# LSH attention followed by a feed-forward layer: the first batch's hidden layer by seven half-size products, its operands and all weight block sums made during attention

## The chip, the cores and the metric

The kernel runs on one core of a Trainium2 chip. The metric is the device time of one execution in microseconds (us). The engines are called as in the profile: PE multiplies matrices and writes PSUM, ACT, DVE and POOL work element by element, and SP issues nearly all DMAs. Each engine takes its instructions strictly in order; engines wait for each other through semaphores.

## The reference

Attention runs over 4 batches, 8 heads, 768 tokens and head size 64. Queries and keys are hashed to 6 bits each by the signs of a projection, and a query attends only to the keys of its own bucket. Its output, laid out as 3072 tokens by 512, goes through a feed-forward layer of 2048 hidden values with a piecewise quadratic activation:

```python
q_bits = (np.einsum('bhsd,dk->bhsk', q, proj) > 0)
k_bits = (np.einsum('bhsd,dk->bhsk', k, proj) > 0)
mask = q_bucket[:, :, :, None] == k_bucket[:, :, None, :]
scores = np.where(mask, scale * np.matmul(q, k.transpose(0, 1, 3, 2)), -1e9)
attn = softmax(scores)                  # with 1e-9 added to the sum
x = np.matmul(attn, v)                  # as 3072 x 512
h = x @ w_in                            # 512 x 2048
g = np.where(h >= 1, h, np.where(h <= -1, 0.0, (h + 1) ** 2 / 4))
out = g @ w_out                         # 2048 x 512
```

The weights arrive as 64-bit floats. Every product that needs more than the matrix format's precision is made of three: each operand is split into a high part and a rest, and high by high, rest by high and high by rest are summed.

## The kernel before

**Attention** (`attention`) goes through 32 heads, a pair of heads at a time, in units: a unit is 128 keys by 384 queries, so a head has 12 units and the stage has 384. At unit g, PE makes the scores (lines 378, 379), ACT takes the exponential twice (line 387 rounded to the matrix format, line 392 in full), and one unit later DVE, or POOL for two units in six, subtracts the two and so makes the rest `pl` (line 39 through `lo_unit`). Four units behind, PE multiplies by the values (`pv_unit`, lines 411, 413, 415). For the head after next, PE makes one pair of `smax` products every two units (line 310) into a single buffer, and DVE reduces the buffer to row maxima (line 314); the next pair can be made only when that reduction is done. Everything else is a task that is put behind a numbered unit (`at(g, fn)`), in the order of the code.

**Weights.** A block of 128 hidden values (an f, of which there are 16 for w_in and 16 for w_out) is converted from 64-bit floats by a load, a rescaling on ACT (`rebias`, line 66) and three integer steps on DVE (`tail`, `shifted`, `signed`, lines 70, 74, 78), which use a PSUM bank as scratch. For 12 blocks of w_in, ACT then makes the high part and POOL the rest, into a large resident tile `wbig`. Twelve more blocks (4 of w_in, 8 of w_out) are converted in attention and put to DRAM to be split later. So heads 3 to 26 each carry one conversion.

**Feed-forward.** The tokens go by chunks of 384, two chunks to a batch. The hidden layer of the first batch (chunks 0 and 1) is made directly: 32 steps (`ffn_order`, `gemm1`, line 976) of 12 products for one chunk and one f. The other three batches use the seven-product scheme of Strassen's kind on 2 by 2 blocks (`PRODUCTS`): for a pair of f's and both chunks, seven half-size products of 6 matmuls each (line 1071) give four results that would otherwise take eight such products. Seven block combinations of the weights (`wc`, in DRAM) and of the tokens are its operands; a ring of buffers holds the weight blocks that come next. The results are combined on DVE and ACT (`cm`, `cu`, `cv`, lines 1076 to 1090), go through the activation (`act_in` on ACT, `act_out` on DVE), are split by `g_hi` and `g_lo`, and wait in a list as nine output matmuls each (`queue_out`, line 839, 512 wide). `issue(n)` takes the next n from that list, five or six behind each product.

While the first batch ran in the old way, DVE also made the weight block sums (`w_get`, `w_sum`, `w_hi`, `w_lo`, `w_put`) and the token operands of batch 1 (`x_plan`). The token operands of chunk 0 were made in heads 28 to 31 (`make`: two DVE steps, a POOL copy and a POOL subtraction per block of 128), those of chunk 1 in the first steps of the feed-forward stage.

Two PSUM banks, `h0` and `h1`, take the products in turn. A product that starts afresh in a bank, or accumulates onto the one before it there, has to wait until the engine that reads the earlier result has read it.

Of the kernel before, what the change touches and what calls it, by code (L numbers as in the profile page):

```python
# [41 lines left out]
class WeightSplit:  # L42
# [10 lines left out]
    def steps(self, src, shape, hi, lo, cp, stage=None, low=None, keep=None, word=None):  # L53
        nc, n = self.nc, self.n
        st = {}

# [7 lines left out]
        def rebias():  # L64
            st["sq"] = self.pool.tile([P, n], F32, name="wsq")
            nc.scalar.activation(out=st["sq"], in_=st["raw"][:, :, 1].bitcast(F32), func=AF.Copy, scale=REBIAS)

        def tail():
            a = st["a"] = self.pool.tile([P, n], I32, name="wa", bufs=1) if word is None else word()
            nc.vector.tensor_scalar(out=a, in0=st["raw"][:, :, 0], scalar1=29, scalar2=None,  # L70
                                    op0=ALU.logical_shift_right)
# [10 lines left out]
        def s5():  # L82
            if cp is nc.scalar:
                cp.copy(out=hi, in_=st["sq"])
            else:
                cp.tensor_copy(out=hi, in_=st["sq"])

        def s6():
            sub(nc, low or nc.gpsimd, lo, st["sq"], hi.bitcast(F32))

        def put():
            nc.sync.dma_start(out=keep if stage is None else stage, in_=st["sq"])

        if stage is None:
            return [s0, rebias, tail, shifted, signed, s5, s6] + ([put] if keep is not None else [])

        def get(sq=None):
            st["sq"] = self.pool.tile([P, n], F32, name="wsq") if sq is None else sq
            nc.sync.dma_start(out=st["sq"], in_=stage)

        return [s0, rebias, tail, shifted, signed, put], [get, s5, s6]


# [551 lines left out]
LEAD = 8  # L655
# [7 lines left out]
NRING = 9  # L663
# [3 lines left out]
class XMaker:  # L667
# [23 lines left out]
    def load_sv(self, c, sv):  # L691
        self.sv[c] = sv
        self.nc.sync.dma_start(out=sv, in_=self.x_d[c // 2][:, :, S:S + 2])

# [6 lines left out]
    def load_er(self, c, ct, er):  # L701
        self.load_rows(c // 2, ct, c % 2, er)
        self.er[c, ct] = (er[:, 0], er[:, 1])

    def load_raw(self, c, ct, raw):
        b, sl = c // 2, slice(c % 2 * CH, (c % 2 + 1) * CH)
        self.nc.sync.dma_start(out=raw, in_=self.x_d[b][:, ct, sl])
        self.raw[c, ct] = raw

    def make(self, c, ct, part, hi, lo, eng):  # L710

        nc = self.nc
        r, sv = self.raw[c, ct], self.sv[c]
        eb, rb = self.er[c, ct]
        if part == 0:
            nc.vector.scalar_tensor_tensor(out=r, in0=eb, scalar=sv[:, ct, 0:1], in1=r,
                                           op0=ALU.mult, op1=ALU.add)
        elif part == 1:
            eng[0].tensor_tensor(out=r, in0=r, in1=rb, op=ALU.mult)
        elif part == 2:  # L720
            (nc.scalar.copy if c > 0 else nc.gpsimd.tensor_copy)(out=hi[:, ct], in_=r)
        else:
            sub(nc, eng[1], lo[:, ct], r, hi[:, ct].bitcast(F32))


def ffn_order():


    steps = [(0, f) for f in range(LEAD)]
    for f in range(NFT):  # L730
        steps.append((1, f))
        if f + LEAD < NFT:
            steps.append((0, f + LEAD))
    return steps


def ffn(ctx, tc, wpair, woh, wol, xm, xa, xb, areas, wst, wq, wc, out, prep, post, staged):
# [12 lines left out]
    nc.vector.memset(m1, -1.0)  # L750
    pcs = xp.tile([P, 6, CH], F32, name="pcs")
    pc = [pcs[:, n] for n in range(6)]
    tmp = xp.tile([P, 2, 4, HM], F32R, name="tmp")
    sum_w = xp.tile([P, 4, HM], F32, name="sumw")
    sflat = sum_w.rearrange("p b n -> p (b n)")
    spc = (xp.tile([P, NCT, 2], F32, name="xsva"), xp.tile([P, NCT, 2], F32, name="xsvb"))
    xs = [xa, xb]
    N1 = 2 * NFT
    (ta, tb, tu), big = areas
    tflat = tmp.rearrange("p a b n -> p (a b n)")  # L760

    def cut(t, n):
        return t[:, n * CH:(n + 1) * CH]
# [3 lines left out]
            + [cut(big, n) for n in range(28, 32)] + [cut(tflat, n) for n in range(5)]  # L767
            + [cut(tu, n) for n in range(3)])

    def operand(b, o, cc, t):  # L770
        return sets[(b - 1) % 2][cc * 2 * NBLK + 2 * o + t]

    def spread(b, cc, k):

        if b == 2:
            t, n = (ta, 2 * k) if cc == 0 else ((tb, 6), (big, 28), (big, 30), (tu, 0))[k]
        elif b == 3:
            t, n = big, 2 * NBLK * cc + 2 * k
        else:
            t, n = (ta, 2 * k) if cc == 1 else (tflat, 2 * k) if k < 2 else (sflat, 0) if k == 2 else (  # L780
                pcs.rearrange("p k n -> p (k n)"), 4)
        return t[:, n * CH:(n + 2) * CH].bitcast(F32).rearrange("p (t n) -> p t n", t=2)
# [6 lines left out]

    def mid(n, fn, *a):  # L790

        (prep if n < N1 else post)[n].append((fn, a))

# [22 lines left out]

    def flush(c, m):
# [64 lines left out]
    def x_plan(b, cc, raw, er, norm, made):  # L882

        at(raw, x_raw, b, cc)
        for k, n in enumerate(norm):
            mid(n, x_norm, b, cc, k)
            at(er[k], x_er, b, cc, k)
# [64 lines left out]
    def ring_staged():  # L952
# [4 lines left out]
        for k in range(4):  # L957
            w_load(k)
# [346 lines left out]
```

## Time and profile before

| | |
|---|---|
| median of 3 runs | 968.71 us (968.69 to 968.91) |
| the profiled execution | 968.67 us, of which the span of its instructions is 966.7 us |
| granted PE clock | 0.999 |
| PE, matmuls | 956.6 us busy, 5050 of them |
| DVE, ACT, POOL busy | 747.8, 680.4 and 322.4 us |
| attention | up to 450.55 us of the span |
| first batch's direct steps | 450.55 to about 578.7 us |

Matmuls of PE overlap: one that shows 0.34 us is followed by the next 0.175 us after its start, so the pace is read from the distance of starts, or from the chain of waits, and not from the durations. The same is true on a smaller scale for ACT and DVE, whose instructions start some 0.1 us ahead of the end of the one before.

### The profile page before, as it was taken

How to read it: one execution, taken by the hardware profiler on the slowest of the kernel's cores; microseconds unless marked ns; L12 is line 12 of the kernel's file. 1: busy time of each engine (PE TensorE's matmuls, PEld its weight loads, DVE VectorE, ACT ScalarE, POOL GpSimd, SP SyncE). 2: the span in 40 equal slices, each digit the busy share in tenths (PEclk: the TensorE clock that was granted, in tenths of full speed). 3: DMA queues.
4: the chain of work that ended last, by engine and by line, in shares of the span. 5: the costliest groups of instructions: out<-in, count | busy, mean ns of one | idle time of the engine just before them, and what ended most of it. 6: DMA issues, size and time to landing. Idle time of an engine off the chain costs nothing.

```text
span 966.7 us, 15568 instructions
## 1 busy us (share of the span) xinstructions
PE 956.6 (99%) x5050; PEld 889.8 (92%) x5050; DVE 747.8 (77%) x1313; ACT 680.4 (70%) x1482; POOL 322.4 (33%) x433
## 2 busy tenths in 40 slices
PE   8999999999999999999999999999999999999998
PEld 7899999999999999999889998888998899888996
DVE  8778889888888888885988787787866777655554
ACT  7789999999999999987655465555564545544444
POOL 8777776666677776476000000000000000000000
PEclk9999999999999999999999999999999999999999
DMA  5776656666766666636691669966458554454431
GB/s 160 191 190 161 167 163 181 180 182 201 193 188 172 172 169 169 146 106 166 193 346 45 196 209 314 306 215 190 120 181 217 159 174 120 145 151 119 121 87 65
DMA packets 95112, 167.55 MB, mean 173 GB/s; under 512 B 13956, under 2 KB 51960, under 8 KB 95032
## 3 DMA queue, kind: packets, MB, share of 16 engines
q1 hardware_dynamic: 94762, 166.53, 60.3%
q8 instruction: 40, 0.66, 0.3%
q14 instruction: 40, 0.33, 0.1%
q10 hardware_dynamic: 270, 0.04, 0.0%
HBM read 106.13 MB, written 33.87 MB: 145 GB/s over the span
## 4 chain that ended last, share of the span: by engine, by line
PE 94%; DVE 2%; ACT 1%; issue 0%; ACTq 0%; DVEq 0%
PE y L839 27%; PE h L1071 18%; PE h L976 7%; PE smax L310 7%; PE o L411 7%; PE o L415 7%; PE s L378 7%; PE o L413 7%; PE s L379 6%; PE o L208 2%; DVE nm L314 1%; ACT ph L387 0%; ACT t L798 0%; ACT z L799 0%; PE s L355 0%
## 5 line engine op out<-in xcount | busy, mean ns | idle before, releaser
L387 ACT ACTIVATE ph<-s 128x384 fp32r<-128x384 f32 x380 | 189.7, 499 | 32.7 <-PE s L379 25.2
L314 DVE TENSOR_REDUCE nm<-smax 128x1 f32<-128x768 f32 x189 | 179.6, 950 | 22.5 <-PE smax L310 22.1
L39 DVE TENSOR_TENSOR pl<-s,ph 128x384 fp32r<-128x384 f32 x256 | 137.5, 548 | 28.8 <-ACT s L392 27.8
L39 POOL TENSOR_TENSOR pl<-pf,ph 128x384 fp32r<-128x384 f32 x128 | 129.8, 1014 | 88.2 <-ACT pf L392 85.0
L804 DVE SCALAR_TENSOR_TENSOR t<-t 128x384 f32<-128x384 f32 x128 | 71.3, 557 | 106.4 <-ACT z L799 106.3
L378 PE MATMUL s<-t 128*128 128x384 f32 x384 | 130.5, 340 | 0.0
L411 PE MATMUL o<-ph,va 128*128 128x386 f32 x384 | 130.1, 339 | 0.2 <-DVE neg L219 0.2
L413 PE MATMUL o<-ph,vb 128*128 128x386 f32 x384 | 129.9, 338 | 0.0
L415 PE MATMUL o<-pl,va 128*128 128x386 f32 x384 | 129.9, 338 | 0.0
L379 PE MATMUL s<-t 128*128 128x384 f32 x384 | 129.5, 337 | 0.0
L392 ACT ACTIVATE s<-s 128x384 f32<-128x384 f32 x252 | 126.2, 501 | 0.0
L839 PE MATMUL y<-t,ghi 128*128 128x512 f32 x384 | 124.7, 395 | 0.0
L310 PE MATMUL smax<-t 128*128 128x384 f32 x378 | 99.3, 344 | 2.6 <-DVE nm L314 2.0
L798 ACT ACTIVATE t<-h,mh 128x384 f32<-128x384 f32 x56 | 32.5, 581 | 83.3 <-PE h L976 43.8
L809 ACT CAST ghi<-z 128x384 fp32r<-128x384 f32 x129 | 65.1, 505 | 30.1 <-DVE z L805 26.3
L799 ACT ACTIVATE z<-t,m 128x384 f32<-128x384 f32 x128 | 79.0, 617 | 4.2
L839 PEld LDWEIGHTS y<-t,ghi 128*128 128x128 f32 x384 | 71.3, 188 | 11.1 <-ACT ghi L809 0.3
L1071 PE MATMUL h<-wbig,t 128*128 128x384 f32 x399 | 81.4, 336 | 0.0
L798 ACT ACTIVATE t<-wsq,mh 128x384 f32<-128x384 f32 x48 | 29.6, 617 | 67.0 <-DVE wsq L1084 40.8
L1071 PEld LDWEIGHTS h<-wbig,t 128*128 128x128 f32 x399 | 71.6, 188 | 5.3
L839 PE MATMUL y<-t,glo 128*128 128x512 f32 x192 | 76.0, 396 | 0.0
L839 PE MATMUL y<-woh,glo 128*128 128x512 f32 x192 | 75.7, 394 | 0.2
(192 smaller groups left out, 2063.2 us busy)
## 6 DMA issues: line engine op xcount, KB each, us to landing
t<-wc SPq DMA_DIRECT2D x92, 256.0 KB
t<-t SPq DMA_DIRECT2D x60, 384.0 KB
wraw<-wc SPq DMA_DIRECT2D x76, 256.0 KB
raw<-in_qk_dram SPq DMA_DIRECT2D x14, 768.0 KB
wraw<-in_w_in_dram SPq DMA_DIRECT2D x16, 512.0 KB
wraw<-in_w_out_dram SPq DMA_DIRECT2D x16, 512.0 KB
t<-ed SPq DMA_DIRECT2D x36, 192.0 KB
xd<-xs SPq DMA_DIRECT2D x32, 192.5 KB
```

The source lines that it names most:

```text
L39: eng.tensor_tensor(out=out, in0=a, in1=b, op=ALU.subtract)
L310: nc.tensor.matmul(out=smax[hd][:, hf, 0:HS], lhsT=t2[:, 0, h, i * P:(i + 1) * P], rhs=t2[:, 1, h, hf * HS:(hf + 1) * HS], start=True, sto ...
L314: nc.vector.tensor_reduce(out=nmp(hd)[:, i:i + 1], in_=smax[hd][:, :, 0:HS], axis=AX.XY, op=ALU.max, negate=True)
L378: nc.tensor.matmul(out=ps[:, 0:HS], lhsT=t1[:, 1, h, ks], rhs=t1[:, 0, h, sl], start=True, stop=False)
L379: nc.tensor.matmul(out=ps[:, 0:HS], lhsT=t2[:, 1, h, ks], rhs=t2[:, 0, h, sl], start=False, stop=True)
L387: nc.scalar.activation(out=ph[:, 0:HS], in_=ps[:, 0:HS], func=AF.Exp, scale=SCALE)
L392: nc.scalar.activation(out=pf, in_=ps[:, 0:HS], func=AF.Exp, scale=SCALE)
L411: nc.tensor.matmul(out=o, lhsT=wa, rhs=ph, start=(jj == 0), stop=False)
L413: nc.tensor.matmul(out=o, lhsT=wb, rhs=ph, start=False, stop=False)
L415: nc.tensor.matmul(out=o, lhsT=wa, rhs=pl, start=False, stop=(jj == NJ - 1))
L839: nc.tensor.matmul(out=ys[c][m], lhsT=g_[:, m * P:(m + 1) * P], rhs=w, start=(first and k == 0), stop=(last and k == 2))
L1071: nc.tensor.matmul(out=ps, lhsT=w[:, cs], rhs=x, start=(n == 0 and s not in (2, 3, 6)), stop=(n == 5), skip_group_check=True)
```

## The change

All four batches now go through the seven-product loop: `ffn_order`, `gemm1` and the old loop are gone, and the loop's count `NK` is 4 x 56 instead of 3 x 56. For that the operands of batch 0 must be there when attention ends.

- **Weights.** In attention, each pair p of w_in's f's (`weights(p)`, p = 0 to 7) takes three heads from head 3 + 3p: two conversions into a tile `rw`, then splits of the plain blocks, three differences and splits of the four sum blocks. ACT makes four high parts per pair; POOL makes the differences (`diff`) and the rests (`lo`); two DMAs put the pair's seven blocks to `wc`. The third head of the three converts a block of w_out. Three more blocks of w_out follow in heads 27, 28 and 29, so 27 conversions stand in attention where 24 did.
- **Tokens.** `FirstX` makes the seven combinations of batch 0's tokens: for the first half of the features in two passes over 192 columns (heads 13 to 21 and 23 to 28: `fill` on DVE, `norm`, `sums` and `lo` on POOL, `hi` on ACT), for the second half in heads 28 to 31 over 384 columns (`fill` on DVE, `norm` on POOL, and `sums`, `hi` and `lo` all on DVE).
- **Feed-forward.** The ring has 8 slots instead of 9, the first five weight blocks are loaded in heads 29 and 30, and the first six products issue no output matmuls (`issue(0 if k < 6 ...)`). Five conversions of w_out remain in the stage where eight were; `make`, the w_sum steps and `x_plan(1)` of the old stage are gone or moved into the loop.

```diff
-    def w_sum(part):
-        r, t = raw_w.bitcast(F32), sum_w
...
-    for n, (c, f) in enumerate(ffn_order()):
...
-        g = act_in(gemm1(n, c, f))
...
-    for i in range(NW1):
-        conv((2 * i + 3) * NU, wi_steps(i, nc.scalar), (0, 9, 10, 11, 14 - (i == 0), 17, 19, 21))
...
-        conv((4 + 2 * n) * NU, first, (0, 9, 10, 11, 14, 16))
...
-        for part, n in enumerate((14, 18, 19, 20)):
-            at(g0 + n + 6 * ct, xm.make, 0, ct, part, *xa, (nc.vector, nc.gpsimd))
...
+    SUMS = {3: (3, 2, 3, ALU.add), 5: (2, 0, 2, ALU.subtract), 4: (0, 3, 0, ALU.subtract), 6: (1, 1, 0, ALU.subtract)}
...
+    def fill(self, k):
+        r, er, ct = self.pc(k), self.er[k][:, 0, self.sl], 2 * (k % 2) + self.cc
+        self.nc.vector.scalar_tensor_tensor(out=r, in0=er, scalar=self.sv()[:, ct, 0:1], in1=r, op0=ALU.mult,
+                                            op1=ALU.add)
+
+    def norm(self, k):
+        r = self.pc(k)
+        self.nc.gpsimd.tensor_tensor(out=r, in0=r, in1=self.er[k][:, 1, self.sl], op=ALU.mult)
...
+    NK = B * (NFT // 2) * NBLK
...
-        issue(6 if s == 6 else 4 if 3 <= k < 6 else 5)
+        issue(0 if k < 6 else 6 if s == 6 else 5)
...
+    def weights(p):
+        h0, r = 3 + 3 * p, rw[p % 2]
+        f0, f1 = r[:, 0::3], r[:, 1:3]
+        conv(h0 * NU, wi_steps(2 * p, f0), (0, 9, 10, 11, 14 - (p == 0)))
+        conv((h0 + 1) * NU, wi_steps(2 * p + 1, f1), (0, 9, 10, 11, 14))
+        wo_staged(h0 + 2, p)
...
+            at(g + his[n], hi, d, x)
+            at(g + los[n], lo, d, x)
...
+            at(g + subs[n], diff, d, x, y)
...
+            at(g + shis[n], hi, hs[:, sl], r[:, sl])
+            at(g + slos[n], lo, hs[:, sl], r[:, sl])
...
+    for n, gs in enumerate((((13, 2, 5), (13, 3, 7), (15, 2, 5), (15, 3, 10)),
+                            ((23, 2, 5), (23, 3, 7), (25, 2, 4), (25, 3, 5)))):
+        for k, (h, a, m) in enumerate(gs):
+            at(unit(h, a), fx[n].fill, k)
+            at(unit(h, m), fx[n].norm, k)
...
+    for k, n in enumerate((11, 14, 17, 20)):
...
+        at(g0 + n - 1, fx[2].fill, k)
+        at(g0 + n, fx[2].norm, k)
+    for o, n in ((0, 24), (2, 26), (1, 28), (3, 30), (5, 32), (4, 34), (6, 36)):
+        piece(fx[2], o, g0 + n, nc.vector, nc.vector)
```

Here `g0` is the first unit of head 28, and `unit(h, n)` is unit n of head h. In all, 5002 matmuls stand where 5050 did: 56 products of 6 replace 32 steps of 12, which is 48 fewer.

Three places in the order of the instructions matter. The first is DVE in head 30, from the reduction behind unit 0 of that head on. Before:

```order
L314 TENSOR_REDUCE nm_5654<-smax_5752 128x1
L39 TENSOR_TENSOR pl_4_166<-s_5756,ph_4_159 128x384
L716 SCALAR_TENSOR_TENSOR raw_5442<-t2_1_78,xsv0_5443,raw_5442 128x384
L314 TENSOR_REDUCE nm_5654<-smax_5778 128x1
L39 TENSOR_TENSOR pl_5_167<-s_5769,ph_5_160 128x384
L384 CAST ph_0_155<-s_5800 128x384
```

And now, where line 327 is the reduction, line 83 the step `signed`, line 755 the high part of a token operand and the line 39 behind it its rest:

```order
L327 TENSOR_REDUCE nm_5775<-smax_5877 128x1
L39 TENSOR_TENSOR pl_4_159<-s_5882,ph_4_152 128x384
L83 SCALAR_TENSOR_TENSOR wsq_5839<-wsq_5839,wsc_92,o0_130 128x512
L755 CAST wbig_80<-raw_5553 128x384
L39 TENSOR_TENSOR wbig_80<-raw_5553,wbig_80 128x384
L327 TENSOR_REDUCE nm_5775<-smax_5903 128x1
L39 TENSOR_TENSOR pl_5_160<-s_5894,ph_5_153 128x384
L397 CAST ph_0_148<-s_5926 128x384
```

One fill stood between the two reductions; now a conversion step, a copy and a subtraction do. The second place is PE at the end of attention, where the first feed-forward products begin. Before:

```order
L415 MATMUL o1_138<-pl_3_165,va_1_152 128x386
L976 MATMUL h0_6081<-t2_1_78,wbig_80 128x384 x12
L976 MATMUL h1_6082<-t2_1_78,wbig_80 128x384 x12
...
L839 MATMUL y_6201<-t1_2_76,ghi_6142 128x512 x2
```

And now (h0 and h1 are the two PSUM banks, y is an output block):

```order
L428 MATMUL o1_131<-pl_3_158,va_1_145 128x386
L960 MATMUL h0_6202<-wbig_80,t1_1_75 128x384 x6
L960 MATMUL h1_6203<-wbig_80,t1_1_75 128x384 x6
...
L960 MATMUL h1_6203<-wbig_80,t1_2_76 128x384 x6
L960 MATMUL h0_6202<-wbig_80,t1_2_76 128x384 x6
L960 MATMUL h1_6203<-wbig_80,ring_6208 128x384 x6
L960 MATMUL h0_6202<-wbig_80,ring_6208 128x384 x6
L856 MATMUL y_6305<-t1_2_76,ghi_6257 128x512 x2
```

A bank was used again after 12 matmuls of the other; now after 6, seven times in a row with no output matmuls between. The third place is POOL in head 19, between the rests `pl` of units 3 and 9 of that head. Before:

```order
L39 TENSOR_TENSOR pl_0_162<-pf_3852,ph_0_155 128x384
L39 TENSOR_TENSOR pl_3_165<-pf_3899,ph_3_158 128x384
L39 TENSOR_TENSOR pl_6_168<-pf_3938,ph_6_161 128x384
```

And now, where `rw` holds weights and `xq` tokens:

```order
L39 TENSOR_TENSOR pl_0_155<-pf_3897,ph_0_148 128x384
L39 TENSOR_TENSOR wbig_80<-rw0_98,wbig_80 128x2x256
L39 TENSOR_TENSOR wbig_80<-xq_100,wbig_80 128x192
...
L752 TENSOR_TENSOR xq_100<-xq_100 128x192
L39 TENSOR_TENSOR pl_3_158<-pf_3949,ph_3_151 128x384
L39 TENSOR_TENSOR wbig_80<-rw1_99,wbig_80 128x2x256
...
L39 TENSOR_TENSOR pl_6_161<-pf_3993,ph_6_154 128x384
```

POOL had nothing else between these three; now three rests of weights and several token steps stand there.

460 lines of the change are left out of this document (190 added, 270 removed).

## The prediction

> **What bounds the kernel now.** I read the page's busy times first, then busy time by stretches, then the waits of PE.
>
> ```profile
> PE 956.6 (99%) x5050; PEld 889.8 (92%) x5050; DVE 747.8 (77%) x1313; ACT 680.4 (70%) x1482; POOL 322.4 (33%) x433
> ...
> 200.00:225.00 25.00, 25.00 (x145) 24.56 (x144) 21.43 (x34) 23.16 (x56) 17.33 (x23) 1.00 0.62 172
> 425.00:450.00 25.00, 25.00 (x142) 24.48 (x142) 18.23 (x31) 22.20 (x53) 20.32 (x24) 1.00 0.47 122
> 500.00:525.00 25.00, 25.00 (x127) 22.56 (x126) 20.28 (x39) 14.25 (x28) 0.00 (x0) 1.00 0.42 145
> ...
> PE smax L310 <- DVE nm L314: 2.0, 8, 0.4
> ```
>
> The columns of a stretch are its length, then busy time (and count) of PE, weight loads, DVE, ACT and POOL. PE is never idle in the three stretches and its clock is full. DVE makes it wait 2.0 us in all. So PE is the bound in both stages, and a matmul less is worth its pace; but in attention ACT stands at 93%, DVE at 86% and POOL at 69%, and there the change puts its new work. Now the pace, from the chain of waits:
>
> ```profile
> 450.71 8.41 PE h L976 x48
> 459.13 2.10 PE y L839 x9
> 461.23 2.09 PE h L976 x12
> ...
> 576.58 2.10 PE y L839 x9
> ```
>
> Forty-eight matmuls of 384 columns take 8.41 us, 0.1752 each; nine of 512 columns take 2.10. These pieces follow each other without a gap from 450.7 to 578.7: the old first batch loses nothing to waits.
>
> **The change, part by part.** All against the profiled execution's 968.67 us, which lies 0.04 under the median.
>
> *1. Fewer matmuls.* 5002 for 5050, all 48 from the first batch: 48 x 0.1752 = **-8.4 us**. The output matmuls are the same in number, and the list still holds 30 of them at the end, so the end of the kernel is the same. The loop itself is the one of batches 1 to 3.
>
> *2. The start of the loop.* Six products now go first with no output matmuls between, so every PSUM bank is used again after one other product, 6 x 0.1752 = 1.05 us. The latencies, from batch 1 (start, duration):
>
> ```profile
> 618.40 1.22 PE L1071 MATMUL h<-wbig,wraw 128*128 128x384 f32 x6
> ...
> 619.66 0.56 DVE L1084 TENSOR_TENSOR wsq<-h,wa 128x384 f32<-128x384 f32 x1 [0.65 <-PE h L1071]
> 620.25 0.62 ACT L798 ACTIVATE t<-wsq,mh 128x384 f32<-128x384 f32 x1 [1.70 <-DVE wsq L1084]
> ...
> 608.09 0.62 ACT L799 ACTIVATE z<-t,m 128x384 f32<-128x384 f32 x1
> 608.74 0.56 DVE L804 SCALAR_TENSOR_TENSOR t<-t 128x384 f32<-128x384 f32 x1 [1.33 <-ACT z L799]
> 609.33 0.56 DVE L805 TENSOR_TENSOR z<-t,z 128x384 f32<-128x384 f32 x1
> 609.81 0.55 DVE L1090 TENSOR_TENSOR wsq<-h,wsq 128x384 f32<-128x384 f32 x1
> ```
>
> A product's result is read 1.26 us after its start; an activation takes 0.65 on ACT, twice, before DVE can begin (608.74 against 608.09), and DVE then starts its steps 0.59 and 0.48 apart. Count from the first product. The third, from 2.11, is read by ACT at 3.35, its z ends at 4.6, and DVE's two steps run from 4.65. Only behind them in DVE's order stands the reading of the fourth product (cv), from 5.72 to 6.27; the sixth product needs that bank and would start at 5.26. PE waits 1.05 us. The same happens a round later: the sum cu of the seventh product stands behind another activation and ends near 12.6, while PE reaches the ninth product, which needs its bank, near 12.0: 0.6 more. After that five output matmuls (1.17 us) lie between products and cover it, as they do in batch 1. **+1.7 us**; bounds 0 (the waits overlap with something I miss) and 3.
>
> *3. DVE in heads 28 to 30.* First what DVE can bear, in a stretch of heads 19 and 20:
>
> ```profile
> 253.29 0.75 DVE L74 SCALAR_TENSOR_TENSOR o<-wsq,wsc,o 128x512 int32<-128x512 int32 x1
> 253.95 0.55 DVE L39 TENSOR_TENSOR pl<-s,ph 128x384 fp32r<-128x384 f32 x1
> 254.42 0.94 DVE L314 TENSOR_REDUCE nm<-smax 128x1 f32<-128x768 f32 x1
> 255.28 0.55 DVE L39 TENSOR_TENSOR pl<-s,ph 128x384 fp32r<-128x384 f32 x1
> 255.75 0.74 DVE L78 SCALAR_TENSOR_TENSOR wsq<-wsq,wsc,o 128x512 int32<-128x512 int32 x1
> 256.40 0.95 DVE L314 TENSOR_REDUCE nm<-smax 128x1 f32<-128x768 f32 x1
> 257.27 0.55 DVE L39 TENSOR_TENSOR pl<-s,ph 128x384 fp32r<-128x384 f32 x1
> 258.25 0.66 DVE L683 SCALAR_TENSOR_TENSOR sm<-em,sm 128x48 f32<-128x48 f32 x1 [0.43 <-DMA em<-ed]
> 258.95 0.19 DVE L684 TENSOR_SCALAR sm<-sm 128x48 f32<-128x48 f32 x1
> 259.05 0.95 DVE L314 TENSOR_REDUCE nm<-smax 128x1 f32<-128x768 f32 x1
> 259.92 1.01 DVE L39 TENSOR_TENSOR pl<-s,ph 128x384 fp32r<-128x384 f32 x2
> 260.85 0.95 DVE L314 TENSOR_REDUCE nm<-smax 128x1 f32<-128x768 f32 x1
> ...
> 255.50 0.54 PE L310 MATMUL smax<-t 128*128 128x384 f32 x2
> 257.63 0.51 PE L310 MATMUL smax<-t 128*128 128x384 f32 x2
> 260.06 0.61 PE L310 MATMUL smax<-t 128*128 128x384 f32 x2
> ```
>
> The pitch of a reduction is 0.87, of a rest pl 0.465 (two in 0.93), of the integer steps 0.66 and 0.65. The smax pair of 257.63 was ready at 258.14; its reduction started 0.91 late, and the next pair came at 260.06, 2.43 after the last instead of 2.13. So a reduction may be some 0.6 to 0.7 late for nothing, and beyond that PE waits one for one. The other prices:
>
> ```profile
> L70 DVE TENSOR_SCALAR o<-wraw 128x512 int32<-128x512 int32 x24 | 16.6, 694 | 3.9 <-ACT xs L421 2.6
> ...
> L39 DVE TENSOR_TENSOR wbig<-pcs,wbig 128x384 fp32r<-128x384 f32 x30 | 16.2, 550 | 0.0
> ...
> L175 DVE CAST t<-wraw 128x384 fp32r<-128x384 f32 x2 | 0.7, 374 | 0.1
> ...
> 423.01 0.96 DVE L716 SCALAR_TENSOR_TENSOR raw<-t,xsv,raw 128x384 f32<-128x384 f32 x1
> ...
> L716 DVE SCALAR_TENSOR_TENSOR pcs<-t,xsva,pcs 128x384 f32<-128x384 f32 x4 | 2.4, 612 | 0.0
> ...
> 422.26 1.29 POOL L39 TENSOR_TENSOR t<-wsq,t 128x512 fp32r<-128x512 f32 x1
> ```
>
> Less the overlap of 0.09: tail 0.60, sums and rests of tokens 0.46, a copy 0.28 to 0.37 (I take 0.37, a POOL neighbour being likely), a fill 0.87. Six units of attention with three smax pairs are 36 matmuls, 6.3 us; without pairs 30, 5.3. DVE's sums, by its order: units 345 to 350: four pl, three reductions, the three conversion steps and two fills: 1.86 + 2.61 + 1.91 + 1.74 = 8.1, over by 1.8. Units 351 to 356, with two fills: 6.2, even. Units 357 to 362, with the conversion and two token pieces: 1.86 + 2.61 + 1.91 + 1.66 = 8.0, over by 1.7. Units 363 to 368, with a PSUM copy (0.56), three pieces and two sums: 5.8, over by 0.5. Then 5.0 against 5.3. That makes 4.0; 0.7 is borne by the reductions, and about as much again (an estimate: no row shows it) once they have ended and only the rests are waited for. **+2.7 us.** The check on the method: a window with a conversion and no fill, as at 253 us, sums to 6.4 for 6.3, and PE shows no loss there. Bounds: 0, if later lateness is borne as well, and 9, the second rival below.
>
> *4. The rest of attention.* Eight fills of 192 columns stand in heads 13, 15, 23 and 25, close behind the step `signed`: 6.4 + 2 x 0.4 over 6.3, less the 0.7 borne: 0.2 each time, **+0.8 us** (0 to 3). ACT gets 32 high parts of weights and 14 of tokens, all in odd heads but the few of head 28:
>
> ```profile
> L84 ACT CAST wbig<-wsq 128x512 fp32r<-128x512 f32 x12 | 7.3, 608 | 0.0
> ```
>
> At some 0.5 for 512 columns an odd head gets up to 2.3 us more where ACT idled 7% (0.9); the even heads lose the 0.5 that they had. ACT runs behind PE for a few units and catches up in the even head. POOL gets 60 more instructions, 0.5 to 1.3 us each, and goes from 69% to about 90%; its rests pl are needed five units later, so I cost both at nothing. If that cover goes, 0.3 us in each of 12 odd heads is 3.6. The three conversions of heads 27 to 29 are in part 3. DMAs: SP issues 708 for 703, the block sums go out in attention instead of later, and the DMA share is 0.62 there; nothing.
>
> *5. The loop with less DVE work.* The block sums leave DVE. By its order, only the three groups of seven products with the late w_out conversions ask 16 us of DVE against 15.8 of PE; a lateness of 0.5 in all is borne. Nothing.
>
> Sum: -8.4 + 1.7 + 2.7 + 0.8 = **-3.2**, 968.67 - 3.2 = **965.5 us**.
>
> **The rivals.**
>
> *The cover holds.* Parts 3 and 4 cost nothing, because DVE is idle 14% of attention and lateness is passed on. For it: a whole conversion per head costs PE nothing now. Against it: the windows above are over by more than the idle share. 968.7 - 8.4 + 1.7 = 962.0; with no wait at the start either 960.3.
>
> *DVE and POOL lock each other out.* The fill at 423.01 took 0.96, ending 0.42 after the POOL subtraction of 422.26 to 423.55; in the feed-forward stage, with POOL silent, the same operation takes 0.61. So DVE seems to wait for POOL's instruction to end. In heads 30 and 31 there are now 18 DVE steps from SBUF to SBUF (7 copies, 7 rests, 4 sums). If each waits half a POOL instruction (0.5), two thirds of the time, that is 6 us more: 971.5, **slower**. It decides from 0.18 us per step on, which would eat the 3.2. Against it: POOL has only some 7 us of work in head 30. The Trainium skill, "SBUF — State Buffer", section "SBUF: two separate sides", says that VectorE and GpSimd share a port pair under an exclusive lock, and that VectorE operations in a two-port mode or with two SBUF inputs are subject to it. By that rule the copies, rests and sums would all wait, not the fills alone; the row at 423.01 agrees for the fill, and no run here shows the others yet.
>
> *ACT or POOL becomes the bound* in the odd heads: 3.6 us more, 969.1, no difference.
>
> *The saving doesn't come*, since DVE bounds the late groups of part 5: each 0.5 to 1 us behind, up to 3: 968.
>
> **How the numbers follow.** Forecast 0.45, cover 0.23, lock 0.16, ACT or POOL 0.1, no saving 0.06. The range of 960.8 to 970.8 leaves out the end of the lock and of the cover, 2 in 10. A measurement tells 0.2% (1.9 us) from no change: faster, under 966.8, holds the cover and most of the forecast, 0.62; slower, over 970.6, the lock and a little of the third, 0.18; the same 0.20.
>
> **What would show it.** Right: a first batch of about 121 us (128.0 less 8.4, and 1.7 at its start); waits of PE's line 310 for DVE in heads 28 to 30 of 2 to 3 us; the first nine products with gaps of about 1 and 0.6. Wrong: stretches of heads 13 to 27 with fewer than 144 matmuls in 25 us (part 4), DVE copies of line 755 of 0.6 us or more (the lock), or no gap at the start.

## The result, and the profile after

Slower. The changed kernel takes 1008.03 us (median of 4 runs, 1004.12 to 1010.10) against 968.81 for the kernel before beside it: a ratio of 1.040 (95% interval 1.036 to 1.044). The prediction was 965.5, with 970.8 as its upper end; the sign was wrong, and the size by 42 us. The profiled run is the one of 1004.12, with a span of 1002.3 us. Its first lines, the busy time of the engines, and stretches as in the prediction (PE, weight loads, DVE, ACT, POOL, clock, DMA share, GB/s):

```profile
PE 962.1 (96%) x5002; PEld 882.5 (88%) x5002; DVE 755.8 (75%) x1325; ACT 684.3 (68%) x1503; POOL 369.1 (37%) x493
...
175.00:200.00 25.00, 19.90 (x105) 19.33 (x105) 16.45 (x26) 17.18 (x42) 16.37 (x23) 0.93 0.90 261
200.00:225.00 25.00, 25.00 (x144) 24.50 (x143) 22.43 (x36) 23.64 (x58) 18.98 (x22) 1.00 0.79 223
250.00:275.00 25.00, 21.33 (x118) 20.22 (x118) 18.62 (x31) 21.04 (x52) 20.32 (x28) 1.00 0.73 193
450.00:475.00 25.00, 19.74 (x107) 17.90 (x105) 24.24 (x39) 17.20 (x42) 12.16 (x15) 1.00 0.37 116
500.00:525.00 25.00, 25.00 (x126) 22.45 (x125) 17.97 (x35) 13.97 (x27) 0.00 (x0) 1.00 0.85 236
575.00:600.00 25.00, 21.61 (x103) 17.75 (x102) 21.15 (x41) 12.31 (x23) 0.00 (x0) 1.00 0.55 180
```

The 48 matmuls are gone, and PE is idle where it never was: ten of the twelve stretches of 25 us from 150 to 450 us have 105 to 140 matmuls where 142 to 145 stood. The first feed-forward product starts at 486.86 us, 36.3 later than before (450.55); from there to the end it takes 515.4, only 0.7 less than before (516.15). (Lines of this kernel's attention stand 13 below those printed above: the row of maxima is made at 368 and sent at 375, the pairs of `smax` at 323.) What PE waited for, and how long (us in total, times, longest):

```profile
PE smax L323 <- DVE nm L327: 10.5, 15, 3.2
PE s L392 <- DMA t<-te: 6.0, 3, 5.1
PE s L368 <- POOL nmr L359: 5.8, 8, 1.2
PE o L428 <- DVE pl L39: 4.2, 5, 2.5
PE h L960 <- DVE cu L979: 3.4, 3, 1.5
...
PE h L960 <- DVE cv L971: 0.9, 1, 0.9
```

These are five kinds of wait (the two lines of `h` are one kind), which before had 2.0 us between them. Reading the starts of the matmuls, I count gaps of 0.25 us or more: 7.0 us before line 368, 6.5 before 392, 8.5 before 323 up to head 28, 6.6 in heads 29 to 31, and in the feed-forward layer 1.7 at the start and 4.9 at 567 to 601. That is 35 of the 44 us that are lost (35.6 more span, and 8.4 saved). The clock, below, takes some 3.4 more, and the rest must be shorter gaps.

Four places show how. **The clamp**: two short POOL steps (lines 357 and 359) bring a head's maxima into the form that PE turns into a row (line 368). The timeline of POOL, of DVE and then of PE around 375 us (start, duration):

```profile
372.90 0.51 POOL L163 CAST t<-raw 128x384 fp32r<-128x384 f32 x1
373.49 1.01 POOL L39 TENSOR_TENSOR t<-raw,t 128x384 fp32r<-128x384 f32 x1
374.44 0.51 POOL L163 CAST t<-raw 128x384 fp32r<-128x384 f32 x1
375.04 1.00 POOL L39 TENSOR_TENSOR t<-raw,t 128x384 fp32r<-128x384 f32 x1
376.00 0.24 POOL L357 TENSOR_SCALAR nmr<-nm 128x6 fp32r<-128x6 f32 x1
376.20 0.24 POOL L359 TENSOR_SCALAR nmr<-nm 128x6 fp32r<-128x6 f32 x1
...
374.44 0.96 DVE L327 TENSOR_REDUCE nm<-smax 128x1 f32<-128x768 f32 x1 [0.36 <-PE smax L323]
...
376.49 0.23 PE L368 MATMUL s<-ident_r,nmr 128*12 128x128 f32 x1 [1.21 <-POOL nmr L359]
```

POOL works without a pause and has the splitting of the next keys ahead of the two clamps. PE has the row in its order two units behind them, so it stands and waits. **The sync queue**, issues of SP, then PE:

```profile
177.37 1.70 SPq L735 DMA_DIRECT2D xq<-xd  x2
179.11 0.44 SPq L66 DMA_DIRECT2D wraw<-in_w_out_dram  x1
180.95 1.35 SPq L714 DMA_DIRECT2D wbig<-ed  x2
183.01 0.65 SPq L299 DMA_DIRECT2D vraw<-in_v_dram  x1
183.76 0.65 SPq L438 DMA_DIRECT2D xd<-xs  x1
184.47 0.43 SPq L439 DMA_DIRECT2D sd<-xs  x1
184.95 1.24 SPq L714 DMA_DIRECT2D wbig<-ed  x2
186.73 0.80 SPq L375 DMA_DIRECT2D t<-te  x1
...
191.82 0.69 PE L392 MATMUL s<-t 128*128 128x384 f32 x1 [5.10 <-DMA t<-te]
192.30 0.53 PE L424 MATMUL o<-ph,va 128*128 128x386 f32 x1
192.62 0.53 PE L426 MATMUL o<-ph,vb 128*128 128x386 f32 x1
192.95 0.52 PE L428 MATMUL o<-pl,va 128*128 128x386 f32 x1
```

ACT had made the row at 180.95; its 3 KB stood behind the token loads, were issued 5.8 us later, and landed 11 us after they were made. And behind the pause the matmuls start 0.325 us apart in place of 0.175. **The clock** in stretches of 5 us (last columns as above):

```profile
185.00:190.00 5.00, 1.72 (x10) 1.39 (x8) 3.16 (x6) 2.41 (x6) 3.05 (x4) 1.00 0.89 232
190.00:195.00 5.00, 3.18 (x10) 3.18 (x11) 0.85 (x1) 1.09 (x3) 1.45 (x2) 0.68 0.51 132
195.00:200.00 5.00, 5.00 (x30) 4.92 (x29) 3.73 (x7) 4.29 (x11) 4.45 (x8) 0.98 1.03 313
```

**DVE and POOL in heads 29 to 31**, DVE's rows and POOL's:

```profile
466.31 1.67 DVE L752 TENSOR_TENSOR raw<-raw 128x384 f32<-128x384 f32 x1
468.88 0.55 DVE L39 TENSOR_TENSOR pl<-s,ph 128x384 fp32r<-128x384 f32 x1
471.12 1.51 DVE L39 TENSOR_TENSOR wbig<-raw,wbig 128x384 fp32r<-128x384 f32 x1
...
466.28 1.28 POOL L39 TENSOR_TENSOR t<-wsq,t 128x512 fp32r<-128x512 f32 x1
468.65 1.17 POOL L39 TENSOR_TENSOR pl<-pf,ph 128x384 fp32r<-128x384 f32 x1 [1.09 <-ACT pf L405]
470.95 1.26 POOL L39 TENSOR_TENSOR t<-wsq,t 128x512 fp32r<-128x512 f32 x1
```

Both long DVE steps end 0.42 us after the POOL step that had begun before them, as the fill in the prediction did. The rest of 468.88, which reads PSUM, runs beside the POOL step of 468.65 and takes its usual 0.55.

### The profile page after: what moved, and what is told of

Read it like the earlier page. It is cut to its first block, busy times and chain, and to the rows that moved or that the text cites. A ratio compares the mean times of both kernels' runs of the same rounds, so it can differ in the third digit from the quotient of the medians.

```text
span 1002.3 us, 15608 instructions
## 1 busy us (share of the span) xinstructions
PE 962.1 (96%) x5002; PEld 882.5 (88%) x5002; DVE 755.8 (75%) x1325; ACT 684.3 (68%) x1503; POOL 369.1 (37%) x493
## 4 chain that ended last, share of the span: by engine, by line
PE 66%; DVE 10%; POOL 8%; ACT 6%; DMA 4%; issue 2%; SPq 1%; ACTq 0%; POOLq 0%; DVEq 0%
PE y L856 23%; PE h L960 20%; PE smax L323 4%; PE s L392 4%; PE s L391 4%; PE o L424 3%; PE o L428 3%; PE o L426 3%; POOL t L39 2%; PE o L221 2%; POOL pl L39 2%; DVE nm L327 2%; ACT ph L400 1%; DVE t L817 1%; DVE z L818 1%
## 5 line engine op out<-in xcount | busy, mean ns | idle before, releaser
L960 PE MATMUL h<-wbig,t 128*128 128x384 f32 x420 | 84.5, 337 | 3.6 <-DVE cu L979 3.4
L323 PEld LDWEIGHTS smax<-t 128*128 128x128 f32 x378 | 65.7, 190 | 23.8 <-DVE nm L327 21.0
L960 PEld LDWEIGHTS h<-wbig,t 128*128 128x128 f32 x420 | 74.8, 188 | 10.6 <-DVE cu L979 4.7
L392 PEld LDWEIGHTS s<-t 128*128 128x128 f32 x384 | 72.9, 190 | 7.2 <-DMA t<-te 7.0
L428 PEld LDWEIGHTS o<-pl,va 128*128 128x128 f32 x384 | 73.2, 191 | 6.2 <-DVE pl L39 6.0
```

Of the source, the lines that this page charges most:

```text
L323: nc.tensor.matmul(out=smax[hd][:, hf, 0:HS], lhsT=t2[:, 0, h, i * P:(i + 1) * P], rhs=t2[:, 1, h, hf * HS:(hf + 1) * HS], start=True, sto ...
L392: nc.tensor.matmul(out=ps[:, 0:HS], lhsT=t2[:, 1, h, ks], rhs=t2[:, 0, h, sl], start=False, stop=True)
L428: nc.tensor.matmul(out=o, lhsT=wa, rhs=pl, start=False, stop=(jj == NJ - 1))
L960: nc.tensor.matmul(out=ps, lhsT=w[:, cs], rhs=x, start=(n == 0 and s not in (2, 3, 6)), stop=(n == 5), skip_group_check=True)
```

## The experiments

Theories: **A**, POOL is behind and makes the clamp late; **B**, the sync queue and the landing are late; **C**, the lock between DVE and POOL; **D**, mere load on DVE; **E**, the order of DVE's steps in the feed-forward layer; **F**, ACT's time. The edits are against the changed kernel. "Attention" is the start of the first feed-forward product, "the rest" the span from there, both of the profiled run; the kernel before ran beside all of them at 968.6 to 969.1.

| kernel | median us | ratio (95%) | attention | the rest |
|---|---|---|---|---|
| before | 968.8 | 1 | 450.6 | 516.2 |
| changed | 1008.03 | 1.0400 (1.0364 to 1.0436) | 486.9 | 515.4 |
| e1_te_late | 1077.05 | 1.1114 (1.1098 to 1.1131) | 560.0 | 515.5 |
| e2_te_act | 1005.99 | 1.0385 (1.0369 to 1.0400) | 489.4 | 515.5 |
| e3_no_diffs | 1000.84 | 1.0335 (1.0318 to 1.0353) | 482.5 | 515.5 |
| e4_nmr_dve_te_act | 1001.30 | 1.0337 (1.0310 to 1.0365) | 484.1 | 515.5 |
| e5_nmr_te_sums | 997.88 | 1.0302 (1.0287 to 1.0317) | 480.3 | 515.5 |
| e6_split_dve_low_pool | 1008.61 | 1.0406 (1.0390 to 1.0423) | 485.0 | 519.0 |
| e7_fx2_act_act_later | 997.17 | 1.0287 (1.0271 to 1.0303) | 485.2 | 507.4 |
| e8_no_token_pool | 1002.76 | 1.0347 (1.0330 to 1.0365) | 485.5 | 515.6 |
| c1_fixes | 984.94 | 1.0163 (1.0146 to 1.0180) | 476.4 | 507.0 |
| c2_fixes_spread | 986.74 | 1.0183 (1.0168 to 1.0198) | 478.8 | 507.0 |
| c5_spread_te_sync | 978.73 | 1.0100 (1.0083 to 1.0117) | 469.2 | 507.0 |
| c4_fixes_no_pool | 985.63 | 1.0171 (1.0156 to 1.0186) | 477.1 | 506.9 |
| d1_loads_apart | 996.01 | 1.0278 (1.0259 to 1.0297) | 475.8 | 515.6 |
| d2_act_later | 997.18 | 1.0293 (1.0272 to 1.0313) | 490.5 | 507.3 |
| d3_loads_later | 983.34 | 1.0152 (1.0137 to 1.0167) | 474.3 | 507.0 |
| d4_no_pool_sync | 978.40 | 1.0100 (1.0083 to 1.0117) | 469.5 | 507.0 |
| f1_no_pool_copies | 976.06 | 1.0078 (1.0061 to 1.0095) | 465.9 | 507.1 |
| f2_loads_apart_hs_pool | 979.05 | 1.0105 (1.0090 to 1.0120) | 470.3 | 507.0 |

**e1: the row three units later.**

```diff
-(g + NU + SHIFT - 1, g + NU + SHIFT + 1)
+(g + NU + SHIFT - 1, g + NU + SHIFT + 4)
```

> One number is changed: the product that turns a head's maxima into a row (line 368) and the row's copy come 3 units (about 3 us) later, so GpSimd's clamp (line 359) has 5 units instead of 2. If GpSimd is merely behind by up to 1.4 us there (theory A), the eight waits of line 368 (7.0 us of gaps) go to under 0.5 and the span falls by 5 to 7 us: about 1000 (profiled 997 to 999). The row then leaves for DRAM and T2 3 us later, so theory B (the sync queue is behind) expects the wait of line 392 in head 11 to stay or to grow from 5.3 to up to 8 us. If the lateness is VectorE's reductions and not GpSimd's (rival), the waits of line 368 stay at 5 us or more.

The waits on POOL went, and the cure cost 69 us where a gain of 5 to 7 was expected:

```profile
PE s L392 <- DMA t<-te: 69.3, 18, 8.6
```

PE needs the row 7 units after line 368 (in head 11 of the changed kernel it was made at 180.95 and wanted at 186.6, 5.6 us later), and the issue and the landing already used that time up: three units less, and 18 heads wait. The pauses also pull the clock down, to 0.958 in the mean. So a late clamp can't be given more time at the cost of the row.

**e2: the row's DMA on ACT's queue. e3: POOL's block sums left out. e4: the clamp on DVE, and the row on ACT's queue.**

```diff
-(nc.sync if hd > 4 else nc.scalar).dma_start(      # e2, e4
+nc.scalar.dma_start(
-at(gc, max_clamp, hd + 2, nc.gpsimd)               # e4
+at(gc, max_clamp, hd + 2, nc.vector)
-at(g + subs[n], diff, d, x, y)                     # e3
+pass
```

> The row's DMA (line 375) is issued by ScalarE for all heads, so it is no longer behind the token loads on the sync queue. Theory B (the wait of 5.3 us in head 11 is the place in the sync queue: issued at 186.7 though ready at 181.0) expects the wait of line 392 to fall from 6.5 us in all to under 1, and with it the 39 missing matmuls of 175 to 200 us to come back but for a few; span down by 6 to 8: about 1001. If the bandwidth is what is late (DMA share 0.90 there), the row still lands late: wait of 3 us or more. Theory A expects the waits of line 368 unchanged (6 to 7 us).

The wait of line 392 went as B had it, and the time hardly moved (2 us): in 175 to 200 us PE has 129 matmuls for 105, and 2 to 8 fewer in eight other stretches of attention. A part of it came back at once in head 11: PE now waited 2.3 us there for the next load that stands behind the token loads on the sync queue (line 295, `t<-bits`). c5 gives the other part.

> Leaves out the differences and sums of the first layer's weight blocks (the three subtractions of each pair of weights on GpSimd); everything else, their rests too, is still made, of other numbers. GpSimd's busy time falls by about 22 us. Theory A (GpSimd has too much) expects the waits of line 368 to fall from 7 to under 3 us, and span down by 4 to 8: about 1002. If those waits come from the order on GpSimd alone and not from its load, they stay at 6 or more and the time stays within 2 us of 1008. Nothing of it touches head 11's wait of 5.3 us (theory B).

7.2 us less, with a wait of 4.2 us left in head 11 (5.1 before): A, though line 368 still waits 4.3 us in all, more than the 3 that A expected.

> Two edits: the clamp of the maxima (line 359) goes from GpSimd to VectorE, and the row's DMA to ScalarE. Theories A and B together expect both kinds of wait gone (7 and 6.5 us) and the clock's fall after the long pause with them: 1008 less 13 to 17, about 993. If VectorE's own waits take their place (it waited for loads and for GpSimd in heads 15 to 28, 8.5 us of late reductions), the gain is half of that: about 1000.

Half of what was expected came: the clamp now stood behind DVE's own waits, 2.4 us in head 17 and 1.7 in head 25. In the changed kernel this is the row of DVE that made PE wait 3.2 us, and the reason stands in it:

```profile
273.66 0.21 DVE L702 SCALAR_TENSOR_TENSOR sm<-em,sm 128x48 f32<-128x48 f32 x1 [3.36 <-DMA em<-ed]
```

**e5: the sums six units later, too.**

```diff
-at(g + 7, xm.sums_add)
+at(g + 13, xm.sums_add)
```

> The two edits of the run before (clamp on VectorE, row's DMA on ScalarE: 1001.3) and a third: the sums of heads 16 and 24 are added 6 units later (line 702), when their two loads have surely landed. If VectorE's wait for these loads is what now makes the clamp late (theory B: waits of line 368 of 2.6 and 1.8 us in heads 17 and 25, where VectorE stood at line 702), both go, with the clock's fall behind them: 995 to 997. If it is VectorE's load or its waits for GpSimd (theory C), waits of 1.5 us or more come back in the same heads behind other instructions: 1000 to 1002.

Both waits went, 3.4 us gained: B also for these loads.

**e6: GpSimd's splits of heads 29 and 30 to ACT and DVE; in the feed-forward layer DVE's weight rests to GpSimd.**

```diff
-ws.split(back, woh[f], wol[f], nc.gpsimd, nc.gpsimd)   # heads 29, 30
+ws.split(back, woh[f], wol[f], nc.scalar, nc.vector)
-ws.split(back, woh[f], wol[f], nc.scalar, nc.vector)   # feed-forward
+ws.split(back, woh[f], wol[f], nc.scalar, nc.gpsimd)
```

> Two edits in places far apart. First: the splitting of two tiles of output weights in heads 29 and 30 leaves GpSimd (two casts of 0.68 and two rests of 1.27 us) for ScalarE (casts) and VectorE (rests, two of about 0.68). Theory C (a VectorE instruction with both operands in SBUF waits until a GpSimd instruction has ended: 1.67, 1.51, 0.85 us where alone it takes 0.55) expects the waits of line 428 in heads 29 to 31 to fall from 4.2 to 2.5 or less although VectorE gets 1.4 us more. A mere load on VectorE (theory D) expects them to grow by 1.4, to 5.5. Second: in the feed-forward layer the rests of the output weights (0.68 us on VectorE, 14 of them) go to GpSimd, idle there. Theory D (VectorE's load sets the waits of the late groups, 4.9 us at 567 to 601) expects them under 1.5 and the span 3.5 down; theory C expects each GpSimd rest of 1.27 us to hold VectorE up for as long, so that waits stay at 4 us or grow. By C alone about 1006 to 1009, by D in both places 1006.

C, in both places. With more work, DVE in heads 29 to 31 makes PE wait 2.3 us for `pl` and not 4.2; with less work for DVE, the feed-forward layer takes 3.5 us longer. PE waits there for DVE as before and never for GpSimd's new rests, and a DVE step of 0.55 beside one of them takes 1.65:

```profile
564.21 1.65 DVE L887 TENSOR_TENSOR pcs<-pcs 128x384 f32<-128x384 f32 x1
...
563.82 1.63 POOL L39 TENSOR_TENSOR wol<-wsq,woh 128x512 fp32r<-128x512 f32 x1 [12.02 <-ACT woh L96]
```

**e7: the last token pieces on ACT and GpSimd; the activation's DVE steps behind the next product's sum. d2: the second edit alone.**

```diff
-piece(fx[2], o, g0 + n, nc.vector, nc.vector)      # e7
+piece(fx[2], o, g0 + n, nc.scalar, nc.gpsimd)
-        for n in (3, 2, 1):                        # e7, d2: main loop
+        for n in (3, 2):
...
+        due(1, k)        # behind the sums of product k
         for fn, a in post.pop(k, ()):
```

> Two edits in places far apart. First: the pieces of the second half of the tokens' columns in heads 28 to 31 are made with ScalarE (copies) and GpSimd (sums and rests) in place of VectorE. VectorE loses 7 copies, 7 rests and 4 sums, some 10 us. Theory D (load) expects the 6.6 us of gaps in 460 to 476 to fall to 1 or 2; theory C (lock) expects that the 11 GpSimd instructions of about 1 us hold up VectorE's rests and fills, so that 3 us or more stay. Second: in the feed-forward layer VectorE's two steps of an activation (lines 817 and 818), which wait for ScalarE, are written behind the sum of the next product in place of ahead of it. If the waits of the late groups come from that order (VectorE idle for 1.33 us in front of line 817 while the sum of line 979 stands behind it: theory E), they fall from 4.9 to under 2 us; if from VectorE's load alone, they stay. Both as A to E would have it: about 1000.

> The changed kernel with VectorE's two steps of an activation behind the sum of the next product, nothing else. Theory E expects the feed-forward layer without gaps: 6.6 us (4.9 of the late groups, 1.7 of the start) off the span, 1001 to 1002, and attention as it was.

The feed-forward part went from 515.4 to 507.4 and 507.3 us. All of its gaps went but one of at most 0.5, those of the start that the prediction had worked out too: 8.8 us less than before, the saving in full. (The medians fell by 10.8. The runs of the changed kernel go from 1004.1 us at a mean clock of 0.996, the profiled one, to 1010.1 at 0.988, so a part of that can be the clock's.) E is shown: d2 changes the order alone and takes no work from DVE. In heads 29 to 31 e7 left gaps of about 3 of the 6.6 us, as C expected. The medians of e7 and d2 are alike (997.2), so the first edit gained nothing that a median shows.

**e8: GpSimd's token work left out.**

```diff
+if self.cc == 1:     # norm
-piece(fx[n], o, unit(h, m), nc.scalar, nc.gpsimd)
+at(unit(h, m), fx[n].hi, o, nc.scalar)
...
+for n in (9, 11, 13):
+    at(unit(20, n), nc.gpsimd.memset, cut(wbig, n).bitcast(F32), 0.0)
```

> Leaves out GpSimd's part of the first half of the tokens' columns in heads 13 to 28: the products with the inverse sums (8 of 0.61 us), the window sums and the rests (22 of about 0.6); the loads, the fills and ScalarE's copies stay. GpSimd loses about 18 us in 16 heads. Theory A (GpSimd is behind) expects the waits of line 368 to fall from 7 to 3 us or less, as much as without the weights' differences (which left 5.3), and the sync queue's wait in head 11 (5.3 us), which lies ahead of all of this, to stay: about 1001 to 1003. If what the token passes cost is their loads and not GpSimd's work (theory B), the time stays within 2 us of 1008.

5.3 us less, the waits of line 368 down to about 1: A, as for e3.

**c1, c2, c5, c4: the edits together.** c1 has e5's three, e7's two and the first of e6. c2 also sets the token loads apart (the four of head 22 too); c5 is c2 with the row on the sync queue again; c4 is c1 without GpSimd's new work.

```diff
-at(unit(10, 10), fx[0].load, k)
-at(unit(11, 0) + 4 * k, fx[0].rows, k)
-at(unit(22, 2), fx[1].load, k)
+at(unit(*((9, 10), (9, 13), (10, 10), (10, 13))[k]), fx[0].load, k)
+at(unit(*((11, 4), (11, 10), (11, 13), (12, 10))[k]), fx[0].rows, k)
+at(unit(22, 2) + 2 * k, fx[1].load, k)
```

> All edits that helped, in one kernel: clamp on VectorE, row's DMA on ScalarE, sums 6 units later, the last pieces on ScalarE and GpSimd, the output weights' splits of heads 29 and 30 on ScalarE and VectorE, the activation's steps behind the sums. If their gains add (1008.0 to 997.9 is 10.1 for the first three, 1008.0 to 997.2 is 10.8 for the next but the splits), 985 to 987, still slower than before (968.8). If they share a cause, 988 to 992.

> The same with the token loads of heads 10 and 11 set apart (four of 1 us of issue, eight of 0.65, two to eight units from each other, none at the unit at which a row leaves). Theory B expects the wait of 2.4 us in head 11 (there VectorE waits 2.8 us for a weight tile that the sync queue issued late) to go: 2 to 4 us under the kernel beside it. If it is the moves that wait for GpSimd, at which the sync queue stands, the time is within 1 us.

> As the kernel with the token loads set apart, but the row's DMA is issued by the sync queue again. If the loads in one bunch were what held the row up in head 11, the wait of line 392 there stays under 1 us with the sync queue too, and the time is within 1 us of the kernel beside it; if the sync queue is late in general, waits of 2 us or more come back.

> The kernel with all edits that helped, and GpSimd's new work left out: the weights' differences and the first half of the tokens' products with the inverse sums, window sums and rests (loads, fills, ScalarE's copies stay). If GpSimd's work is what is left of the loss in attention (theory A, with the lock of theory C), attention comes within 4 us of before (first feed-forward product at 450.6 there) and the whole under before: 962 to 968. If ScalarE's copies and the loads count as much, 970 to 976.

c1 came where the sum of the gains put it. The three others missed (c5 in its time alone), and for one reason: with the row on the sync queue (c5) the kernel is 8.0 us faster than with the row on ACT's (c2), though PE waits 5.2 us for the row, 2.4 of it in head 11 again. ACT's rows of c2 with a row of PE, and the same place of ACT in c5:

```profile
358.38 0.26 ACT L373 CAST te<-s 12x128 fp32r<-12x128 f32 x1 [0.30 <-PE s L368]
358.67 0.70 ACTq L375 DMA_DIRECT2D t<-te  x1
359.42 0.49 ACT L400 ACTIVATE ph<-s 128x384 fp32r<-128x384 f32 x1 [0.77 <-PE s L392]
...
358.41 0.33 PE L392 MATMUL s<-t 128*128 128x384 f32 x1
...
350.36 0.26 ACT L373 CAST te<-s 12x128 fp32r<-12x128 f32 x1 [0.42 <-PE s L368]
350.77 0.49 ACT L400 ACTIVATE ph<-s 128x384 fp32r<-128x384 f32 x1 [0.15 <-PE s L392]
```

An issue takes ACT 0.70 us, in which it makes no exponential: the score that the exponential of 359.42 reads was done at 358.74. 27 heads of that are 18.9 us on an engine with 93% of attention in use. The issue is the one thing that c2 and c5 do differently; as I read it, it also took the rest of e2's gain. Whether it also hid in c4 what GpSimd's work was worth is what d4 asks.

**d1: only the token loads apart and the sums later. d3: c5 with more loads moved. d4: c5 without GpSimd's new work.**

> The changed kernel with the token loads of heads 10 and 11 set apart and the sums of heads 16 and 24 added 6 units later, nothing else: no queue and no engine is changed. Theory B (the sync queue's place and the landing are a part of the loss of their own) expects the wait of line 392 in head 11 to fall from 5.3 to 2.5, the waits of 3.4 and 2.0 in heads 17 and 25 to go, and the clock to stay at 1.00: 8 to 12 us, 997 to 1000. If GpSimd's lateness brings the same waits back elsewhere, 1003 or more.

> The fastest kernel so far (978.7) with more loads moved out of the way of the row of maxima: the output weights' loads 6 units later, the token rows of heads 11 and 28 behind the unit at which the row leaves. It has four waits of line 392 left (2.5, 0.9, 0.7, 1.7 us). Theory B expects these under 1.5 us in all: 974 to 976. If the weights' later loads make ScalarE or VectorE wait for them instead, 978 or more.

> The kernel of 978.7 with GpSimd's new work left out (the weights' differences, the first half of the tokens' products, window sums and rests). With the row's DMA on ScalarE this left the time where it was (985.6 against 984.9), while alone these gained 5 to 7 us. If ScalarE, which issued that DMA, set the pace there and hid GpSimd's share (theory F), then with the sync queue it shows again: 971 to 975. If the clamp on VectorE had already taken GpSimd off the path (so that its work is free now), 977 to 979.

d1: 12.0 us from two timing edits; the clock of the profiled run stayed at 1.00. B, with no other edit beside it. d3 cut the waits for the row from 5.2 to 1.5 us and lost 4.6 us of time: DVE now waited for the weights that came later, with it PE (2.9 us at line 424 for DVE's line 83). d4 is c5: once the clamp has left it, GpSimd's 40 us of new work (22 of block sums, 18 of tokens) cost nothing that a median shows. So ACT had hidden nothing of it in c4.

**f1: d4 with ACT's new copies on the freed GpSimd. f2: the token rows behind the row of maxima, and half of ACT's new copies on GpSimd, nothing left out.**

> As the kernel of 978.4 without GpSimd's new work (the weights' differences and the first half of the tokens' products, window sums and rests left out), and with ScalarE's new copies of attention (32 of 0.42 to 0.63 us of weight blocks, 14 of 0.36 of tokens, 23.5 us in all) made by the GpSimd that this has freed. Left on VectorE and the queues: fills, conversions, loads. If ScalarE, busy for 93% of attention before and 23.5 less the 7.3 us of the copies that it had then more now, is what is left of the loss (theory F), attention, which ends at 469.5 us there and at 450.6 before, ends by 458 and the whole is at 964 to 968. If the queue and VectorE are what is left, 975 to 979.

> Nothing left out. The fastest full kernel so far (978.7) with the token rows of heads 11 and 28 behind the unit at which the row of maxima leaves (without the later weight loads, for which VectorE waited 2.9 us), and with half of ScalarE's new copies (16 of 0.63 us, those of the block sums) on GpSimd, which is off the path in that kernel. Theories B and F expect 3 us from the rows (waits of line 392 of 5.2 down to 2) and up to 5 from the copies: 971 to 976. If GpSimd is brought back on the path by 10 us more (and by what it then holds up on VectorE), 978 to 982. Under 968.6 nobody expects it.

ACT's copies are 2.3 us of it, about as much as the intervals leave open, and not 12: F is the smaller part, unless the same copies cost something on GpSimd, which holds DVE up; that was not taken apart. f2 gained nothing, and it did not do what it was to do: PE still waits 5.1 us for the row (5.2 in c5). No kernel beat the one before; the best that computes everything is c5, 1.0% slower (0.8 to 1.2). Of its 18.6 us in attention, lines 392, 323 and 368 show 11.4 as waits (2.0 of them stood in the kernel before too), one fall of the clock is some 1.7, and the rest must lie in short gaps, at 121 to 143 matmuls per stretch. In 200 to 225 us of c5:

```profile
200.00:225.00 25.00, 24.17 (x138) 23.30 (x137) 23.96 (x40) 23.11 (x56) 19.11 (x22) 1.00 0.74 215
```

DVE is at 96% (86% before), with the clamp and the fills, and the DMA share at 0.74 (0.62). f1 leaves these two; which of them holds more was not tried.

## Why the prediction was wrong

*Part 1, -8.4:* right. With E's gaps gone, the first batch takes 119.4 us in d2 (490.45 to 609.83) where 128.0 stood, and the rest is up to 9.1 us shorter than before (516.15 to 507.0 in c1).

*Part 2, +1.7:* right to the tenth: gaps of 1.05 at the sixth product and 0.64 at the ninth. What I didn't see is that the order that makes them is a choice: d2 removes them.

*Part 3, +2.7:* the right place, and too small by a mechanism that stood among the rivals: 6.6 us of gaps. The second rival was true, at about three quarters of its price. Copies of line 755 took 605 ns in the mean (0.37 taken), rests 736 and sums 911 (0.55 taken): over the 18 steps that is 4.4 us and not 6, and 2.7 + 4.4 comes near the 6.6. The rule that the prediction quotes from the Trainium skill, "SBUF — State Buffer", section "SBUF: two separate sides", says that steps with two SBUF inputs wait for the lock; the rows at 466 and 471 agree, and the one at 468.88, with an input in PSUM, does not wait. My argument against the rival, that POOL had little work left in head 30, missed that the little it had were steps of 0.6 to 1.3 us, one beside each long DVE step.

*Part 4, +0.8:* **the step that failed.** Two sentences of it. "its rests pl are needed five units later, so I cost both at nothing" looked at one product of POOL's and not at the two clamps, which PE needs two units later, in order, and which cannot be given more time (e1). POOL went from some 69% to 78 and 82% (200 to 300 and 300 to 400 us), less than the 90 that I had worked out, and still they came late in eight heads: 7.0 us of gaps, some 5 to 7 of the time by e3 and e8. And "DMAs: SP issues 708 for 703 ... nothing" counted issues and not where they stand: eight new ones stand just ahead of a 3 KB row with 5.6 us to spare. The queue's bunch and two sums that waited for their loads were 12.0 us (d1), clock included. ACT, costed at nothing too, was worth 2.3 (f1). The 3.6 kept as the price "if that cover goes" was of the right kind for POOL and ACT, at about half of what they cost; the queue had no price at all. These steps are not the whole of it: c5, with edits for all of them but ACT's copies, still loses 18.6 of the 36.3 us of attention. Its waits are the same kinds in small, DVE is fuller there (the clamp is on it now), and what the greater part of the 18.6 comes from stays open.

*Part 5, 0:* wrong by 4.9. It asked for DVE's load, and the load was not what made the gaps (d2 takes none of it away, and they go): a late step feeds itself. DVE waits for ACT's z, ACT for DVE's cv, and cu stands behind both. Once late, a round lost up to 1.6 us, until the order was changed.

Of the three signs listed for "wrong", two showed: stretches under 144 matmuls, and copies of 0.6. The third, no gap at the start, did not.

## What to carry to other kernels

Where every engine runs at 70 to 95%, don't ask whether an engine has room for new work, but which of its small products another engine needs soonest, and how late that may be: here two clamps of 0.23 us and a row of 3 KB set much of the time, and 40 us of added work on GpSimd cost nothing that a median shows once the clamps were out of its way. Count a queue's issues where they stand in its order, not in total. And when an engine that waits for another stands in front of a third one's work, writing the two in the other order can be worth more than any load taken off.

## What the runs showed of the hardware

The clock falls after a pause, in steps of 3.4 us. Around two falls of the changed kernel (columns as above):

```profile
188.40:191.80 3.40, 0.00 (x0) 0.00 (x0) 1.52 (x3) 0.50 (x2) 0.00 (x0) 0.99 0.37 78
191.80:195.20 3.40, 3.38 (x11) 3.38 (x12) 0.96 (x1) 1.29 (x4) 1.63 (x3) 0.50 0.69 198
273.70:277.10 3.40, 1.37 (x8) 1.38 (x9) 3.37 (x6) 0.37 (x1) 2.29 (x3) 1.00 0.82 258
277.10:280.50 3.40, 3.40 (x12) 3.40 (x11) 1.90 (x4) 1.98 (x6) 1.28 (x2) 0.50 0.35 116
280.50:284.00 3.50, 3.50 (x21) 3.50 (x21) 2.98 (x5) 3.50 (x10) 2.64 (x4) 1.00 0.93 279
```

A fall costs about 1.7 us (an estimate: 3.4 us at 0.50). With no wait over 1.5 us (the profiled runs of d1 and d3) the clock stayed at 1.00. Waits of 1.8 to 3.2 us had it fall in some runs and not in others: one of 1.8 in e3 did (434.9 us), one of 2.4 in f1 did not (189.2 us). The Trainium skill, "TensorE: Matmul & The Clock Gate", section "Part 1: The HAM clock gate", says that a free-running window of about 3.4 us without work halves the clock. The 0.50 and the 3.4 us agree, 0.325 against 0.175 us per matmul nearly so, and a free-running window fits the scatter. But the window need not be without work: PE made 8 matmuls from 273.7 to 277.1, and the clock fell all the same.

- A DMA issue on ACT's queue takes 0.70 us of ACT's own time (358.67 in c2), which the busy time doesn't count.
- In the rows shown the lock lasts for POOL's whole instruction, and DVE's step then ends 0.42 us later (423.01, 466.31, 471.12); a DVE step with an input in PSUM isn't held up (0.55 beside POOL, at 468.88).
